# Batch 2's q^T by the DMA crossbar with batch 3's loads gated behind it, in place of batch 0's q in two halves

## The chip, the cores and the metric

The kernel runs on one core of a Trainium2 chip. The metric is the device time of one execution in microseconds (us). TensorE is called PE here (PEld its weight loads), VectorE DVE, ScalarE ACT, GpSimd POOL, SyncE SP. Loads from memory that also convert fp32 to fp16 are issued by POOL; output stores and crossbar transposes are issued by SP.

## The reference

Linformer attention, followed by a two-matrix maxout layer and an output projection:

```python
# q, k, v: (8 batches, 8 heads, 1024 tokens, 64); E, F: (64, 1024)
k_proj = np.einsum('ks,bhsd->bhkd', E, k)
v_proj = np.einsum('ks,bhsd->bhkd', F, v)
scores = scale * np.matmul(q, k_proj.transpose(0, 1, 3, 2))     # scale = 1/8
attn = np.exp(scores - max); attn = attn / (sum(attn) + 1e-09)
attn_out = np.matmul(attn, v_proj)

x = attn_out, heads side by side: (8192, 512)
h1, h2 = x @ w1, x @ w2                                         # (512, 1024) each
out = np.maximum(h1, h2) @ w_out                                # (1024, 512) -> float32
```

The kernel uses max(h1, h2) = relu(h1 - h2) + h2. So it needs the weight difference w1 - w2 (`wd_sb`), and a product M = w2 @ w_out (`m_sb`): out = relu(x @ wd) @ w_out + x @ M. From the second half of batch 0 on, both large products are made by a seven-product scheme on 2 x 2 blocks (p1 to p7 in the code).

## The kernel before

Tokens of a batch are split as 128 partitions x 8 blocks (`NC`). A tile of k, v or q holds a whole batch, 1 MB in fp16, and four such tiles rotate:

```python
kvq = ctx.enter_context(tc.tile_pool(name="kvq", bufs=4))
qtp = ctx.enter_context(tc.tile_pool(name="qtp", bufs=2))

def load(t, n, src, b, h0, h1, c0=0, c1=NC):
    nc.gpsimd.dma_start(
        out=t[n][:, h0:h1, c0:c1],
        in_=src[b, h0:h1].rearrange("h (p c) d -> p h c d", c=NC)[:, :, c0:c1],
    )
```

The first loads. Batch 0's q comes in two halves of the token blocks: the first among k's pieces, the second behind the first quarter of the weights:

```python
for h0 in (0, H // 2):
    for h in (h0, h0 + H // 4):
        load(tiles[0], "k", k, 0, h, h + H // 4)
    load(tiles[0], "q", q, 0, h0, h0 + H // 2, 0, NC // 2)
    ...
for h0 in (0, H // 2):
    load(tiles[0], "v", v, 0, h0, h0 + H // 2)
for f0 in range(0, DF, 256):
    for w_sb, w in ((w2_sb, moe_w2), (w1_sb, moe_w1)):
        for z in range(2):
            nc.gpsimd.dma_start(...)          # columns f0 to f0 + 256
    if f0 == 0:
        load(tiles[0], "q", q, 0, 0, H, NC // 2, NC)
nc.gpsimd.dma_start(out=wo_sb, ...)
```

Steps of attention. `step_kv` projects k and v with E and F on PE. `step_qt` turns q on PE and copies the result out of PSUM on DVE; `step_qt_dma` has the same done by the DMA crossbar; `step_gate` is a small POOL copy that keeps what POOL issues behind it until the named tile is there:

```python
def step_qt(t, h0, nh=2, i0=0, i1=NI, att=False):
    qt_ps = att_banks(FP16)[:, 0, :] if att else mm_bank(FP16)
    ...                                        # nh * (i1 - i0) transposes of 128 x 128
    nc.vector.tensor_copy(out=t["qt"][...], in_=qt_ps[...])

def step_qt_dma(t, h0=0, h1=H):
    nc.sync.dma_start_transpose(out=t["qt"][:, h0:h1]..., in_=t["q"][:, h0:h1]...)

def step_gate(t, n="kpt"):
    nc.gpsimd.tensor_copy(out=junk, in_=t[n][0:1, H - 1, 0:1])
```

`step_sc` makes scores and their exponentials for one group (g: four heads, j: half of the tokens), `step_dn` the sums of these and their logarithm on ACT, `step_inv` the inverse, `step_at` the values and the scaled result in `xt` (two multiplies on DVE). `step_wd` makes a quarter of w1 - w2 on DVE. `up_slots(t, j)` gives eight slots for half j of batch 0 (u0 and u1 below), each a block of 128 columns of relu(x @ wd); two slots share one quarter of wd. `step_w2t` turns w2, `step_m` makes M.

The head of the program, with `warm(n)` for n idle products that keep PE at work:

```python
step_kv(t, 0, 4, "k"); warm(2)
step_kpt(t, 0, 4); warm(2)
step_qt(t, 0, 4, 0, NI // 2); warm(2)
step_sc(t, 0, 0); warm(2)
step_kv(t, 4, 8, "k")
step_dn(t, 0, 0); step_inv(t, 0, 0); warm(2)
step_kpt(t, 4, 8); warm(4)
step_qt(t, 4, 4, 0, NI // 2); warm(2)
step_sc(t, 1, 0)
step_kv(t, 0, 4, "v")
step_dn(t, 1, 0); step_inv(t, 1, 0)
step_at(t, 0, 0); warm(4)
step_kv(t, 4, 8, "v")
step_at(t, 1, 0); warm(4)
step_wd(0)
load_all(tiles[1], 1, "k", k)

slots = [
    (0, u0[0]), (1, u0[1]), (None, f(step_qt, 0, 4, 2, 4)), (None, f(step_qt, 4, 4, 2, 4)),
    (None, wt[0]), (None, f(step_sc, 0, 1)), (None, f(step_sc, 1, 1)),
    (None, wd[1]), (2, u0[2]), (None, f(step_dn, 0, 1)), (None, f(step_inv, 0, 1)), (3, u0[3]),
    (None, f(step_dn, 1, 1)), (None, f(step_inv, 1, 1)), (None, wt[1]),
    (None, f(step_at, 0, 1)), (None, wd[2]), (4, u0[4]), (None, f(step_at, 1, 1)), (5, u0[5]),
    (None, lambda: loads(1, "v", "q", "k")), (None, wt[2]),
    (None, wd[3]), (6, u1[0]), (7, u1[1]), (8, u0[6]), (9, u0[7]), (None, wt[3]),
    (10, u1[2]), ...
    *((16 + n, lambda n=n: step_m(n)) for n in range(NDC)),
]
```

Then come the units, one for each half batch. A unit n works off the down products of half batch n (pieces "P"), the up products of half batch n + 1 (slots "U", n, h, i, with h the first or second half of the unit) and attention of a later batch in between (slots "G", n, h). Batch 1's attention stands in unit 0, batch 2's begins in unit 1:

```python
t = tiles[2]
at_slot(("P", 0, 6, 0), new_attn, t)
at_slot(("G", 1, 0), step_kv, t, 0, H, "kv", True)
at_slot(("G", 1, 0), loads, 3, "q", "v")
at_slot(("U", 1, 0, 1), step_kpt, t, 0, H, True)
for i, key in enumerate((("U", 1, 0, 0), ("U", 1, 0, 3), ("U", 1, 0, 5), ("U", 1, 1, 5))):
    at_slot(key, step_qt, t, 4 * (i % 2), 4, i // 2 * 2, i // 2 * 2 + 2, True)
for b in range(3, B):                          # n = 2 * b - 3
    at_slot(("G", n, 0), step_qt_dma, t, 0, H // 2)
    at_slot(("G", n, 0), step_qt_dma, t, H // 2, H)
    at_slot(("U", n, 0, 1), step_kv, t, 0, H, "kv", True, True)
    at_slot(("U", n, 0, 6), step_gate, t)
    at_slot(("U", n, 0, 6), loads, b + 1, "k", "v", "q")
```

The scores of batch 2's first group stand at slot ("G", 1, 1), those of its second at ("G", 2, 0).

Of the kernel before, what the change touches and what calls it, by code (L numbers as in the profile page):

```python
# [16 lines left out]
def kernel(  # L17
# [48 lines left out]
    def att_banks(dtype=FP32):  # L66
# [9 lines left out]
            name=nc.get_next_instruction_name(),  # L76
# [21 lines left out]
        alloc(t, n)  # L98
        load(t, n, src, b, 0, H)

    def load(t, n, src, b, h0, h1, c0=0, c1=NC):
        nc.gpsimd.dma_start(
            out=t[n][:, h0:h1, c0:c1],
            in_=src[b, h0:h1].rearrange("h (p c) d -> p h c d", c=NC)[:, :, c0:c1],
        )

    tiles = {b: {} for b in range(B)}
    for n in ("k", "q", "v"):
        alloc(tiles[0], n)
    for h0 in (0, H // 2):  # L110
        for h in (h0, h0 + H // 4):
            load(tiles[0], "k", k, 0, h, h + H // 4)
        load(tiles[0], "q", q, 0, h0, h0 + H // 2, 0, NC // 2)
        if h0 == 0:
            ident = const.tile([128, 128], FP32)
            make_identity(nc, ident)
    for h0 in (0, H // 2):
        load(tiles[0], "v", v, 0, h0, h0 + H // 2)

    w1_sb = big(1).rearrange("p (r f) -> p r f", r=NDC)  # L120
    w2_sb = big(2).rearrange("p (r f) -> p r f", r=NDC)
    wo_sb = const.tile([128, NFB, DM], FP16)
    for f0 in range(0, DF, 256):
        for w_sb, w in ((w2_sb, moe_w2), (w1_sb, moe_w1)):
            for z in range(2):
                nc.gpsimd.dma_start(
                    out=w_sb.rearrange("p (g z) f -> p g z f", z=2)[:, :, z, f0 : f0 + 256],
                    in_=w.rearrange("(g p z) f -> p g z f", p=128, z=2)[:, :, z, f0 : f0 + 256],
                )
        if f0 == 0:  # L130
            load(tiles[0], "q", q, 0, 0, H, NC // 2, NC)
    nc.gpsimd.dma_start(out=wo_sb, in_=moe_w_out.rearrange("(r p) f -> p r f", p=128))

    ones16 = const.tile([128, 512], FP16)
# [4 lines left out]
    def warm(n):  # L139
        w_ps = mm_bank()  # L140
        for _ in range(n):
            nc.tensor.matmul(  # L142
                out=w_ps, lhsT=ones16[:, 0:128], rhs=ones16, start=True, stop=True
            )
# [89 lines left out]
    def step_qt(t, h0, nh=2, i0=0, i1=NI, att=False):  # L234
        qt_ps = att_banks(FP16)[:, 0, :] if att else mm_bank(FP16)
        ni = i1 - i0
        for h in range(nh):
            for i in range(ni):
                nc.tensor.transpose(  # L239
                    out=qt_ps[:, (h * ni + i) * 128 : (h * ni + i + 1) * 128],  # L240
                    in_=t["q"][:, h0 + h, 2 * (i0 + i) : 2 * (i0 + i) + 2, :],
                    identity=ident16,
                )
        nc.vector.tensor_copy(
            out=t["qt"][:, h0 : h0 + nh, i0 * 128 : i1 * 128],
            in_=qt_ps[:, 0 : nh * ni * 128].rearrange("q (h n) -> q h n", h=nh),
        )
# [56 lines left out]
    def step_sc(t, g, j):  # L304
        sc_ps = att_banks()
        t["ps", g, j] = sc_ps
        score(t, g, j, [sc_ps[:, e, :] for e in range(2)])
        nc.scalar.activation(out=t["ex", g, j], in_=sc_ps, func=ACTF.Exp, scale=scale)

    def step_dn(t, g, j):  # L310
        dn_ps = t.pop(("ps", g, j))[:, :, 0:W]
        sums_into(t, g, j, dn_ps)
        t["ld", g, j] = soft.tile([128, 2, W], FP32, tag="ld", name="ld_sb")
        nc.scalar.activation(out=t["ld", g, j], in_=dn_ps, func=ACTF.Ln)

# [138 lines left out]
    U = {(b, o): {"n": n, "b": b, "o": o, "t": tiles[b]} for n, (b, o) in enumerate(units)}  # L454
# [260 lines left out]
    t = tiles[0]  # L715
# [4 lines left out]
    step_kpt(t, 0, 4)  # L720
    warm(2)
    step_qt(t, 0, 4, 0, NI // 2)
    warm(2)
    step_sc(t, 0, 0)
    warm(2)
    step_kv(t, 4, 8, "k")
    step_dn(t, 0, 0)
    step_inv(t, 0, 0)
    warm(2)
    step_kpt(t, 4, 8)  # L730
    warm(4)
    step_qt(t, 4, 4, 0, NI // 2)
    warm(2)
    step_sc(t, 1, 0)
    step_kv(t, 0, 4, "v")
    step_dn(t, 1, 0)
    step_inv(t, 1, 0)
    step_at(t, 0, 0)
    warm(4)
    step_kv(t, 4, 8, "v")  # L740
    step_at(t, 1, 0)
    warm(4)
    step_wd(0)


# [1 line left out]
    u0, u1 = [*up_slots(t, 0)], [*up_slots(t, 1)]  # L747
# [3 lines left out]

    def loads(b, *names):
        for n in names:
            b_ = b + (n == "k" and b < 3)
            if b_ < B:
                load_all(tiles[b_], b_, n, {"k": k, "v": v, "q": q}[n])

    slots = [
        (0, u0[0]), (1, u0[1]), (None, f(step_qt, 0, 4, 2, 4)), (None, f(step_qt, 4, 4, 2, 4)),
        (None, wt[0]), (None, f(step_sc, 0, 1)), (None, f(step_sc, 1, 1)),  # L760
        (None, wd[1]), (2, u0[2]), (None, f(step_dn, 0, 1)), (None, f(step_inv, 0, 1)), (3, u0[3]),
        (None, f(step_dn, 1, 1)), (None, f(step_inv, 1, 1)), (None, wt[1]),
        (None, f(step_at, 0, 1)), (None, wd[2]), (4, u0[4]), (None, f(step_at, 1, 1)), (5, u0[5]),
        (None, lambda: loads(1, "v", "q", "k")), (None, wt[2]),
        (None, wd[3]), (6, u1[0]), (7, u1[1]), (8, u0[6]), (9, u0[7]), (None, wt[3]),
        (10, u1[2]), (11, u1[3]), (12, u1[4]), (13, u1[5]), (14, u1[6]), (15, u1[7]),
        *((16 + n, lambda n=n: step_m(n)) for n in range(NDC)),
    ]
    slots = [((0, n), x) for n, x in slots]
# [25 lines left out]
    def at_slot(key, s, *a):  # L795
        steps.setdefault(key, []).append(lambda: s(*a))
# [14 lines left out]
    for n, x in enumerate((  # L811
        "kv", "", "kpt", "qt00 qt10", "", "sc00 qt01 qt11", "sc10", "dn00 in00", "sc01",
        "at00 dn10 in10", "sc11", "at10 dn01 in01", "dn11 in11", "at01", "at11",
    )):
        key = ("P", 0, (n - 1) // 2, (n - 1) % 2) if n else (0, 19)
        for name in x.split():
            if name[0] == "k":
                if name == "kpt":
                    at_slot(key, step_kpt, t, 0, H, True)
                else:  # L820
                    at_slot(key, step_kv, t)
                    at_slot(key, loads, 2, "v", "q")
            else:
                g, j = int(name[2]), int(name[3])
                s_ = {"qt": step_qt, "sc": step_sc,
                      "dn": step_dn, "in": step_inv, "at": step_at}[name[:2]]
                at_slot(key, s_, t, *((4 * g, 4, 2 * j, 2 * j + 2) if name[:2] == "qt" else (g, j)))
                if name == "qt11":
                    at_slot(key, loads, 2, "k")
        if n in (1, 5):  # L830
            at_slot(key, step_t, 1, (0, 1) if n == 1 else (2, 3))
        if 6 <= n < 10:
            at_slot(key, sums_x, U[0, 1], ((2, 0, 1, 3)[n - 6],))
# [2 lines left out]
    t = tiles[2]  # L836
    at_slot(("P", 0, 6, 0), new_attn, t)
    at_slot(("G", 1, 0), step_kv, t, 0, H, "kv", True)
    at_slot(("G", 1, 0), loads, 3, "q", "v")
    at_slot(("U", 1, 0, 1), step_kpt, t, 0, H, True)  # L840
    for i, key in enumerate((("U", 1, 0, 0), ("U", 1, 0, 3), ("U", 1, 0, 5), ("U", 1, 1, 5))):
        at_slot(key, step_qt, t, 4 * (i % 2), 4, i // 2 * 2, i // 2 * 2 + 2, True)
    for b in range(3, B):
        t = tiles[b]
        n = 2 * b - 3
# [74 lines left out]
```

## Time and profile before

| | |
|---|---|
| time, median of 3 runs | 338.49 us (336.88 to 339.25) |
| span of the profiled run | 335.1 us |
| busy PE, DVE, ACT, POOL | 322.6, 242.5, 201.6, 39.5 us |
| moved by DMA | 52.09 MB, 155 GB/s on average |
| granted PE clock | 1.00 in every slice |

The profile is of one execution. Its page cuts the span into 40 slices of about 8.4 us; a digit is the busy share of a slice in tenths. The chain is the work that ended last, followed back from the last instruction, by what released each step. A line of the timeline has the start, the duration, the engine (SPq: the queue of SP), the line of the program, the operation with its tiles, and in brackets how long the engine had been idle and what ended that. Time to landing of a DMA counts from its issue.

### The profile page before, as it was taken

The page shows a single profiled execution, that of the slowest core. Times are in us where ns is not written, and L with a number is a line of the kernel's source. Part 1 is how long each engine was busy: PE and PEld are TensorE (multiplying, and loading weights), DVE is VectorE, ACT ScalarE, POOL GpSimd, SP SyncE. Part 2 cuts the span into 40 slices and gives each one's busy share as a digit, 9 for nine tenths or more (in the row PEclk, how much of TensorE's full clock was granted, in tenths as well). Part 3 has the DMA queues.
Part 4 walks back from the last instruction along what each step waited for, and adds up shares of the span by engine and source line. Part 5 has one row for each costly group of instructions (what it writes and reads, how often), then busy time and mean ns, then how long its engine had stood idle before and what let it go on. Part 6 is the DMA issues. An engine that isn't in the chain of part 4 may idle for free.

```text
span 335.1 us, 9093 instructions
## 1 busy us (share of the span) xinstructions
PE 322.6 (96%) x3892; PEld 250.3 (75%) x3892; DVE 242.5 (72%) x430; ACT 201.6 (60%) x358; POOL 39.5 (12%) x58
## 2 busy tenths in 40 slices
PE   8977999999999999999999999999999999999994
PEld 3534446658888788877888788878887888888883
DVE  1354688988686779697878779677967796969572
ACT  2228422653577677766777677767776777764541
POOL 8558002102000030002100030003000000000000
PEclk9999999999999999999999999999999999999999
DMA  8999999999920969985999989996999320202032
GB/s 155 203 196 187 200 207 189 201 220 194 201 86 2 212 100 203 236 185 108 157 241 218 158 124 227 197 200 94 212 223 198 77 97 33 94 33 96 32 127 94
DMA packets 72616, 52.09 MB, mean 155 GB/s; under 512 B 25344, under 2 KB 72448, under 8 KB 72576
## 3 DMA queue, kind: packets, MB, share of 16 engines
q0 software_dynamic: 31472, 28.31, 54.2%
q1 hardware_dynamic: 41104, 23.21, 28.5%
q8 instruction: 30, 0.49, 0.5%
q14 instruction: 10, 0.08, 0.1%
HBM read 57.15 MB, written 16.78 MB: 221 GB/s over the span
## 4 chain that ended last, share of the span: by engine, by line
PE 90%; DVE 6%; issue 1%; ACT 1%; DVEq 0%
PE mm_ps L634 42%; PE mm_ps L556 25%; PE mm_ps L402 4%; PE att_ps L182 3%; PE att_ps L280 3%; PE mm_ps L142 3%; PE mm_ps L268 3%; PE mm_ps L438 2%; PE mm_ps L182 1%; DVE xt_sb L327 1%; PE mm_ps L239 1%; DVE o_sb L658 1%; PE mm_ps L280 1%; DVE gt_sb L571 1%; PE att_ps L268 1%
## 5 line engine op out<-in xcount | busy, mean ns | idle before, releaser
L527 ACT COPY p_sb<-mm_ps 128x512 f32<-128x512 f32 x172 | 97.3, 593 | 48.7 <-PE mm_ps L556 34.7
L634 PEld LDWEIGHTS <-big 128*128 128x128 f16 x768 | 73.2, 98 | 12.3 <-issue 3.7
L634 PE MATMUL mm_ps<-T_sb,big 128*128 128x256 f16 x576 | 78.1, 273 | 0.0
L571 DVE TENSOR_TENSOR gt_sb<-mm_ps,p_sb 128x512 f16<-128x512 f32 x56 | 38.5, 688 | 46.2 <-PE mm_ps L556 46.2
L556 PE MATMUL mm_ps<-big,big 128*128 128x256 f16 x336 | 50.4, 273 | 0.6 <-DVE gt_sb L571 0.6
L556 PEld LDWEIGHTS <-big 128*128 128x128 f16 x448 | 43.8, 98 | 5.8 <-issue 0.7
L634 PEld LDWEIGHTS <-gt_sb 128*128 128x128 f16 x384 | 35.5, 98 | 10.1 <-issue 5.8
L634 PE MATMUL mm_ps<-wo_sb,gt_sb 128*128 128x256 f16 x256 | 42.9, 273 | 0.1
L556 PEld LDWEIGHTS <-wd_sb 128*128 128x128 f16 x336 | 32.9, 98 | 4.2 <-issue 0.4
L556 PE MATMUL mm_ps<-xt_sb,wd_sb 128*128 128x256 f16 x224 | 33.6, 273 | 0.2 <-ACT ex_sb L353 0.2
L353 ACT ACTIVATE ex_sb<-mm_ps 128x512 f16<-128x512 f32 x48 | 26.1, 596 | 9.2 <-PE att_ps L280 7.0
L658 DVE TENSOR_TENSOR o_sb<-mm_ps,p_sb 128x512 f32<-128x512 f32 x32 | 21.9, 685 | 10.7 <-PE mm_ps L634 7.2
L379 DVE TENSOR_TENSOR xt_sb<-att_ps,ld_sb 128x1024 f16<-128x1024 f32 x24 | 29.3, 1219 | 0.1
L634 PE MATMUL mm_ps<-m_sb,xt_sb 128*128 128x256 f16 x128 | 24.4, 273 | 0.0
L606 ACT ACTIVATE gt_sb<-mm_ps 128x512 f16<-128x512 f32 x28 | 16.8, 600 | 8.7 <-PE mm_ps L556 8.7
L517 DVE TENSOR_TENSOR big<-gt_sb 128x1024 f16<-128x1024 f16 x32 | 21.9, 685 | 0.2
L231 POOL COPY junk<-kpt_sb 1x1 f16<-1x1 f16 x5 | 1.3, 251 | 174.4 <-DMA kpt_sb<-kp_sb 174.4
L574 DVE TENSOR_SCALAR gt_sb<-gt_sb 128x512 f16<-128x512 f16 (+1 forms) x56 | 20.3, 363 | 1.9
L634 PE MATMUL mm_ps<-wo_sb,big 128*128 128x256 f16 x128 | 21.5, 273 | 0.0
L634 PE MATMUL mm_ps<-T_sb,gt_sb 128*128 128x256 f16 x128 | 21.5, 273 | 0.0
L634 PEld LDWEIGHTS <-xt_sb 128*128 128x128 f16 x192 | 18.8, 98 | 2.2
L571 DVE TENSOR_TENSOR gt_sb<-p_sb 128x512 f16<-128x512 f32 x28 | 19.1, 682 | 0.0
(87 smaller groups left out, 443.8 us busy)
## 6 DMA issues: line engine op xcount, KB each, us to landing
out_dram<-o_sb SPq DMA_DIRECT2D x63, 256.0 KB, 2.6
k_sb<-in_k_dram POOLq DMA_DIRECT2D x7, 1024.0 KB, 10.7
v_sb<-in_v_dram POOLq DMA_DIRECT2D x7, 1024.0 KB, 17.3
q_sb<-in_q_dram POOLq DMA_DIRECT2D x7, 1024.0 KB, 21.9
big<-in_moe_w_dram POOLq DMA_DIRECT2D x16, 128.0 KB, 6.4
k_sb<-in_k_dram POOLq DMA_DIRECT2D x4, 256.0 KB, 6.3
v_sb<-in_v_dram POOLq DMA_DIRECT2D x2, 512.0 KB, 10.9
wo_sb<-in_moe_w_out_dram POOLq DMA_DIRECT2D x1, 1024.0 KB, 10.0
```

The source lines that it names most:

```text
L182: nc.tensor.matmul(out=kv_ps[r * KP : (r + 1) * KP, 0:n], lhsT=eft[:, i, c, :], rhs=t[w][:, h0:h1, c, :], start=(c == 0), stop=(c == NC - 1),)
L268: nc.tensor.matmul(out=banks[e][pos : pos + Z, h * W : (h + 1) * W], lhsT=t["kpt"][o * D : (o + 1) * D, head, s * Z : (s + 1) * Z], rhs=t[ ...
L353: nc.scalar.activation(out=t["ex", g, j][:, e, :], in_=banks[e], func=ACTF.Exp, scale=scale)
L379: nc.vector.tensor_tensor(out=x_out(t, g, j).rearrange("q z o n -> q o z n"), in0=at_ps.rearrange("q o (z n) -> q o z n", z=2), in1=ld[:, ...
L517: nc.vector.tensor_tensor(out=S(i), in0=x, in1=y, op=op)
L527: copy(out=x, in_=bank)
L556: nc.tensor.matmul(out=bank[:, m * W : (m + 1) * W], lhsT=w_[:, n_, (2 * d + m) * 128 : (2 * d + m + 1) * 128], rhs=a[:, n_, :], start=(n ...
L571: nc.vector.tensor_tensor(out=c_blk(j, c), in0=two(x), in1=two(y), op=ALU.add)
L574: nc.vector.tensor_scalar_max(ap, ap, 0.0)
L606: nc.scalar.activation(out=out, in_=in_, func=ACTF.Relu)
L634: nc.tensor.matmul(out=bank[:, i * CH : (i + 1) * CH], lhsT=a(c)[:, i * 128 : (i + 1) * 128], rhs=w_(c), start=(n is not None and m == (lo ...
L658: nc.vector.tensor_tensor(out=o_sb, in0=two(x), in1=two(y), op=ALU.add)
```

## The change

Two things are exchanged. Batch 0's q is loaded as a whole again, in four pieces among those of k, ahead of v; with it, both halves of the tokens go through transposes, scores and sums before the first weight difference, the weights come in two quarters and a half, and the slots behind are put in another order (u1 begins earlier). In unit 1, q of batch 2 is turned by the crossbar, as in the later batches, so that PE and DVE need not do it; and the three loads of batch 3, which were issued in unit 0 and at the start of unit 1, wait until that transpose has landed, so that the DMA engines are free for it.

```diff
     for h0 in (0, H // 2):
-        for h in (h0, h0 + H // 4):
-            load(tiles[0], "k", k, 0, h, h + H // 4)
-        load(tiles[0], "q", q, 0, h0, h0 + H // 2, 0, NC // 2)
+        for n, src in (("k", k), ("q", q)):
+            for h in (h0, h0 + H // 4):
+                load(tiles[0], n, src, 0, h, h + H // 4)
 ...
-    for f0 in range(0, DF, 256):
+    for f0, f1 in ((0, 256), (256, 512), (512, DF)):
 ...
-        if f0 == 0:
-            load(tiles[0], "q", q, 0, 0, H, NC // 2, NC)
 ...
     step_qt(t, 0, 4, 0, NI // 2)
+    step_qt(t, 0, 4, NI // 2, NI)
     warm(2)
     step_sc(t, 0, 0)
+    step_sc(t, 0, 1)
     warm(2)
     step_kv(t, 4, 8, "k")
     step_dn(t, 0, 0)
-    step_inv(t, 0, 0)
     warm(2)
     step_kpt(t, 4, 8)
+    step_dn(t, 0, 1)
+    step_inv(t, 0, 0)
     warm(4)
     step_qt(t, 4, 4, 0, NI // 2)
+    step_qt(t, 4, 4, NI // 2, NI)
     warm(2)
     step_sc(t, 1, 0)
+    step_sc(t, 1, 1)
     step_kv(t, 0, 4, "v")
     step_dn(t, 1, 0)
     step_inv(t, 1, 0)
     step_at(t, 0, 0)
-    warm(4)
+    step_dn(t, 1, 1)
+    step_inv(t, 0, 1)
     step_kv(t, 4, 8, "v")
+    step_inv(t, 1, 1)
     step_at(t, 1, 0)
-    warm(4)
     step_wd(0)
 ...
-            b_ = b + (n == "k" and b < 3)
+            b_ = b + (n == "k" and b < 2)
 ...
-        (0, u0[0]), (1, u0[1]), (None, f(step_qt, 0, 4, 2, 4)), (None, f(step_qt, 4, 4, 2, 4)),
-        (None, wt[0]), (None, f(step_sc, 0, 1)), (None, f(step_sc, 1, 1)),
-        (None, wd[1]), (2, u0[2]), (None, f(step_dn, 0, 1)), (None, f(step_inv, 0, 1)), (3, u0[3]),
-        ...
+        (0, u0[0]), (None, f(step_at, 0, 1)), (1, u0[1]), (None, f(step_at, 1, 1)),
+        (None, lambda: loads(1, "v", "q", "k")),
+        (None, wd[1]), (2, u1[0]), (3, u1[1]), (4, u0[2]), (None, wt[0]), (5, u0[3]),
+        (None, wd[2]), (None, wt[1]), (6, u1[2]), (7, u1[3]), (8, u0[4]), (9, u0[5]), (None, wd[3]),
+        (None, wt[2]), (10, u1[4]), (11, u1[5]), (12, u0[6]), (13, u0[7]), (None, wt[3]),
+        (14, u1[6]), (15, u1[7]),
 ...
-                if name == "qt11":
-                    at_slot(key, loads, 2, "k")
 ...
     at_slot(("G", 1, 0), step_kv, t, 0, H, "kv", True)
-    at_slot(("G", 1, 0), loads, 3, "q", "v")
     at_slot(("U", 1, 0, 1), step_kpt, t, 0, H, True)
-    for i, key in enumerate((("U", 1, 0, 0), ("U", 1, 0, 3), ("U", 1, 0, 5), ("U", 1, 1, 5))):
-        at_slot(key, step_qt, t, 4 * (i % 2), 4, i // 2 * 2, i // 2 * 2 + 2, True)
+    at_slot(("G", 1, 0), step_qt_dma, t, 0, H // 2)
+    at_slot(("G", 1, 0), step_qt_dma, t, H // 2, H)
+    at_slot(("U", 1, 0, 6), step_gate, t, "qt")
+    at_slot(("U", 1, 0, 6), loads, 3, "k", "v", "q")
```

More of the change, by code (lines that the diff above doesn't have):

```diff
@@ L99, in load_all, with load @@
         load(t, n, src, b, 0, H)
-    def load(t, n, src, b, h0, h1, c0=0, c1=NC):
+    def load(t, n, src, b, h0, h1):
         nc.gpsimd.dma_start(
-            out=t[n][:, h0:h1, c0:c1],
-            in_=src[b, h0:h1].rearrange("h (p c) d -> p h c d", c=NC)[:, :, c0:c1],
+            out=t[n][:, h0:h1],
+            in_=src[b, h0:h1].rearrange("h (p c) d -> p h c d", c=NC),
         )
@@ L116 @@
             make_identity(nc, ident)
-    for h0 in (0, H // 2):
-        load(tiles[0], "v", v, 0, h0, h0 + H // 2)
+    load(tiles[0], "v", v, 0, 0, H // 2)
+    load(tiles[0], "v", v, 0, H // 2, H)
     w1_sb = big(1).rearrange("p (r f) -> p r f", r=NDC)
@@ L126 @@
                 nc.gpsimd.dma_start(
-                    out=w_sb.rearrange("p (g z) f -> p g z f", z=2)[:, :, z, f0 : f0 + 256],
-                    in_=w.rearrange("(g p z) f -> p g z f", p=128, z=2)[:, :, z, f0 : f0 + 256],
-                )
-        if f0 == 0:
-            load(tiles[0], "q", q, 0, 0, H, NC // 2, NC)
+                    out=w_sb.rearrange("p (g z) f -> p g z f", z=2)[:, :, z, f0:f1],
+                    in_=w.rearrange("(g p z) f -> p g z f", p=128, z=2)[:, :, z, f0:f1],
+                )
     nc.gpsimd.dma_start(out=wo_sb, in_=moe_w_out.rearrange("(r p) f -> p r f", p=128))
@@ L758 @@
     slots = [
-        (0, u0[0]), (1, u0[1]), (None, f(step_qt, 0, 4, 2, 4)), (None, f(step_qt, 4, 4, 2, 4)),
-        (None, wt[0]), (None, f(step_sc, 0, 1)), (None, f(step_sc, 1, 1)),
-        (None, wd[1]), (2, u0[2]), (None, f(step_dn, 0, 1)), (None, f(step_inv, 0, 1)), (3, u0[3]),
[L762 to L766, printed above, removed]
+        (0, u0[0]), (None, f(step_at, 0, 1)), (1, u0[1]), (None, f(step_at, 1, 1)),
[4 more added lines that the diff above has]
+        (14, u1[6]), (15, u1[7]),
         *((16 + n, lambda n=n: step_m(n)) for n in range(NDC)),
```

## The prediction

> **What bounds the kernel now.** First the page: engine shares and the slices.
>
> ```profile
> PE 322.6 (96%) x3892; PEld 250.3 (75%) x3892; DVE 242.5 (72%) x430; ACT 201.6 (60%) x358; POOL 39.5 (12%) x58
> ...
> PE   8977999999999999999999999999999999999994
> ...
> DMA  8999999999920969985999989996999320202032
> ...
> PE 90%; DVE 6%; issue 1%; ACT 1%; DVEq 0%
> ```
>
> PE is busy in 96% of the span and carries 90% of the chain. It drops only in the first four slices (to about 33 us); there the DMA row stands at 9 and stays there until about 92 us. So the head waits for transfers and what hangs on them; behind it the kernel is as long as PE's queue. Hence the busy time by stage: from the first weight-difference product to the end of `step_m`, batch 1's attention, unit 1, and two later units of the steady state.
>
> ```profile
> 24.40:53.00 28.60, 26.16 (x226) 12.70 (x228) 19.16 (x33) 13.05 (x19) 7.89 (x10) 1.00 1.28 199
> 53.00:73.30 20.30, 19.63 (x322) 13.19 (x324) 18.06 (x34) 10.40 (x15) 2.63 (x3) 1.00 1.20 199
> 73.30:95.30 22.00, 21.26 (x264) 17.20 (x264) 17.36 (x34) 11.02 (x21) 1.75 (x2) 1.00 0.98 195
> 95.30:131.20 35.90, 35.90 (x459) 29.72 (x457) 27.36 (x49) 25.40 (x49) 2.81 (x4) 1.00 0.61 109
> ```
>
> Columns: stretch, length, busy PE, weight load, DVE, ACT, POOL, granted clock, DMA share, GB/s. Idle PE is length less PE: 2.44, 0.67, 0.74 and 0.00 us. The clock is 1.00 in all. The change can thus gain by taking PE instructions out of unit 1, by starting or filling the head better, and nowhere later. Then the timeline of PE in the head and in unit 1, with DVE and the queues:
>
> ```profile
> 24.42 1.90 PE L402 MATMUL mm_ps<-xt_sb,wd_sb 128*128 128x512 f16 x8 [1.12 <-DVE wd_sb L416]
> ...
> 34.20 1.04 PE L402 MATMUL mm_ps<-xt_sb,wd_sb 128*128 128x512 f16 x4 [2.09 <-DVE wd_sb L416]
> ...
> 79.32 0.68 DVE L244 COPY qt_sb<-att_ps 128x1024 f16<-128x1024 f16 x1
> ...
> 80.66 0.60 PE L556 MATMUL mm_ps<-big,big 128*128 128x256 f16 x4 [0.56 <-DVE gt_sb L571]
> 80.99 0.54 PEld L239 LDWEIGHTS <-q_sb 128*128 128x128 f16 x8
> ...
> 85.57 0.41 PE L268 MATMUL mm_ps<-qt_sb,kpt_sb 64*32 64x256 f16 x16
> ...
> 110.57 5.70 SPq L251 DMA_TRANSPOSE qt_sb<-q_sb  x2
> ```
>
> The 2.09 us gap at 34.20 is the largest behind 24.4: the third weight difference (`step_wd`) stands on DVE behind the late products of batch 0's second half. The 0.56 at 80.66 is DVE arriving late at `gt_sb` in unit 1, with a q^T copy of 0.68 just ahead of it. The last line is what the change asks for in unit 1, as batch 3 already has it.
>
> **What the Trainium skill says.** "TensorE: Matmul & The Clock Gate", Part 4: PE-mode transpose, says that a transpose on TensorE lands in PSUM and needs a DVE copy after it; the trace agrees: each eight of L239 have a 0.68 us copy of L244. "DMA: Bandwidth & Descriptors", Rules for kernel authors, says that a transpose next to ordinary DMAs needs nothing; so the gate on batch 3's loads serves time, not correctness. The same page, Issuing engines are not separate DMA queues, says that all queues end on the same 16 DMA engines and interleave; the trace agrees: a store landed in 2.2 to 2.5 us in the quiet stretch at 90 to 110 us and in 7 to 8 us beside loads at 61 to 79. That is why the gate matters.
>
> **Part one, batch 2's q^T in unit 1.** Removed: four `step_qt`, each 8 transposes on PE. The chain gives such a group 0.45 us (81.26, 83.45, 91.67), so 4 x 0.45 = 1.8 us of PE in a stretch where PE is the bound: all of it counts. Also removed: four DVE copies of 0.68, 2.7 us out of 17.36; off the path, but for the 0.56 gap that one of them helps to make: I count 0.4 of it. Added: two crossbar transposes on SyncE. Do they arrive in time? Batch 2's q is issued at 56.0 and takes 15.7 us to land (the issue's own row): 71.7, just before the slot at about 73. Nothing else is then queued on the loads' side, since k, v and q of batch 3 (issued at 62 and 75 before) now come later. The later pairs took 5.7 us for the first transpose and start 2 to 3 us apart, so from 71.5 to 73 the first half of heads lands at 77 to 79, the second at 79 to 81. The first score (L268) wanted it at 85.57, and comes some 3.5 us earlier now, at 82: 3 us to spare; the second half is wanted only one group later. The output stores behind it on SyncE's queue (78.50 the next) are clear.
>
> **Part two, the gate.** Batch 3's loads start at about 80 instead of 62 and 75. In the steady state the same three, issued from 121.2 on, had the last (q, 21.9 us from 122.9) landed at 144.8, so 23.6 us. From 80 that is 104. Batch 3's q was transposed from 110.57 and its kv projected at 113.65; less some 4 us saved, 106 and 109. Two us to spare, and a late transpose is still 4 us ahead of its score. So the gate costs nothing.
>
> **Part three, the head.** Gone is the splitting of q. All of q (1 MB as fp16) comes ahead of v; all four score groups of batch 0 stand before the first weight difference; eight warm-up products go, and the 16 transposes (0.89), 32 score products (about 0.9) and 16 sum products (about 0.5) that stood behind 24.4 move ahead of it: 2.3 us less PE work there. The price is a later start. The queue moves 1 MB in 5.1 us (k of batch 1 landed at 28.8 + 14.4 = 43.2, v at 29.6 + 18.6 = 48.2). By bytes, 3.0 MB were in by 21.3, 3.5 by 24.0. In the old order v's second half landed at 7.0 + 12.3 = 19.3; now 0.5 MB of q is ahead of it: 21.4. The first weight quarter moves from 21.3 to 24.0. From v on, in durations of the old trace: projection 1.06 to 22.8 with its copy to 23.2, value products to 23.7, two multiplies 1.29 to 25.1, weight difference 0.68 to 25.75. So the first product comes at 25.75, not 24.42: 1.3 later.
>
> Behind it 26.16 - 2.3 = 23.9 us of PE work remain. Idle: the order is u0[0], values (0,1), u0[1], values (1,1), u1[0]; the two pairs of multiplies on DVE (1.29 each) and PE's products run side by side, and u1[0] needs the last multiply: PE is done at 28.35, DVE at 29.75: 1.4 us. The later weight differences have no such wait: the third and fourth quarter, now one piece of rows twice as long, land at 32.3 by bytes, as the last quarter did before, and are wanted at 36. I add 0.4 for small waits. So `step_m` ends at 25.75 + 23.9 + 1.8 = 51.4 instead of 53.0: 1.6 earlier. Batch 1's v (landed 48.2) and q (53.3, wanted at about 55.5) are in by then, so the shift lasts.
>
> **Sum.** Head -1.6, unit 1's PE work -1.8, its gap -0.4: -3.8; with a little for other small gaps in unit 1 (0.74 idle in all), about -4.0. 338.5 - 4.0 = 334.5 us.
>
> **Rivals.** One: the head gets longer. The halves were there to bring v and the first weights sooner, and the first product is 1.3 us later; were the 2.3 us moved ahead not a gain, because the stage then idles on DVE or on the weights, the head would cost up to 1.3: 338.5 + 1.3 - 2.2 = 337.6. For it: DVE has 19.16 busy in 28.6 there and sits in each of PE's two large gaps. Against it: the 2.09 gap was caused by just those late products. Two: the crossbar is late, because q lands with nothing to spare (71.7 against 73) and stores share the engines. Past 82, each us late is a us of PE; at 3 us late the saving of part one is gone: 336.5 to 337. For it: the 15.7 us to landing. Against: the load that competed, k of batch 3, is now behind the gate. Three: the gate makes batch 3 late, its projection then standing at 109. If loads take 30 us instead of 23.6, 1 or 2 us go: 336. Four: DVE, lighter by 2.7 us in unit 1, frees more than I count: at most the rest of 0.74, so 334.
>
> **Range and chances.** The head is the widest term: from +0.5 to -3. Unit 1 is -2.2, with 1 us either way. The three times before spread 2.4 us, so I allow 1 for the measurement: 331.8 to 337.2. Two per cent faster would be 331.7, just outside: 0.11. Two per cent slower, 345.3, needs a transfer that is late by some 10 us: 0.03. Within: 0.86.
>
> **What would show it.** In the changed profile: PE matmuls fewer by the 32 transposes and 8 warm-up products, 3852 of 3892; the first weight-difference product at about 25.8 behind DVE; one gap of 1.4 before u1[0]; `step_m` done near 51.4; in unit 1 two crossbar transposes issued at 71 to 73, landing by 81, no PE wait for `qt_sb` or `kpt_sb`, and the stretch from batch 2's projection to unit 1's end shorter by 2.2; the gate released near 80, no wait in front of batch 3's projection; the later units as long as before (35.8 to 35.9 for two). What would make it wrong: a wait for weights in the head, a score of batch 2 released by the DMA, or a DVE that trails PE between 30 and 53 us.

## The result, and the profile after

The changed kernel takes 332.84 us (median of 4, 332.65 to 333.04), the kernel before 337.87 beside it (median of 4, 336.88 to 339.25): ratio 0.985, 95% interval 0.981 to 0.989. The spans of the profiled executions are 330.9 and 335.1 us, so 4.2 us are there to be found in the traces. The forecast was 334.5 for a kernel before at 338.5, a ratio of 0.988.

From the page of the changed kernel: the engines, then three rows of the slices (PE, granted PE clock, DMA).

```profile
PE 319.5 (97%) x3852; PEld 247.9 (75%) x3852; DVE 239.9 (73%) x426; ACT 201.4 (61%) x358; POOL 37.1 (11%) x56
...
PE   8968999999999999999999999999999999999994
...
PEclk9997999999999999999999999999999999999998
DMA  8999999998994979995998799996999321212132
```

3852 products, 40 fewer. The third slice of PE is lower than before (6 tenths instead of 7), the fourth higher (8 instead of 7); but the fourth has something new: a granted clock of 7 tenths. The same stages as before, cut at the same events (first weight-difference product, projection of batch 1, of batch 2, and the end of unit 1):

```profile
25.20:51.30 26.10, 25.06 (x160) 11.43 (x160) 18.30 (x32) 9.18 (x13) 4.25 (x5) 0.94 1.24 205
51.30:71.60 20.30, 19.64 (x321) 13.20 (x320) 17.85 (x33) 10.39 (x15) 1.76 (x2) 1.00 1.12 205
71.60:91.10 19.50, 19.32 (x231) 15.39 (x231) 14.56 (x30) 10.74 (x20) 2.90 (x4) 1.00 1.06 168
91.10:127.10 36.00, 36.00 (x460) 29.75 (x459) 27.36 (x49) 25.53 (x49) 2.81 (x4) 1.00 0.85 163
```

The first stage is 26.1 long instead of 28.6 and begins 0.9 later; its mean clock is 0.94. The second is as long as before, the third 2.5 shorter with almost no idle PE (0.18 instead of 0.74), the later units unchanged. So the head gives 1.6 and unit 1 gives 2.5. The timeline of the changed kernel at the places that the prediction named:

```profile
25.29 1.89 PE L400 MATMUL mm_ps<-xt_sb,wd_sb 128*128 128x512 f16 x4 [2.09 <-DVE wd_sb L414]
...
30.88 2.32 PE L400 MATMUL mm_ps<-xt_sb,wd_sb 128*128 128x512 f16 x10 [0.95 <-DVE xt_sb L325]
...
70.09 5.20 SPq L249 DMA_TRANSPOSE qt_sb<-q_sb  x2
...
78.03 0.26 POOL L229 COPY junk<-qt_sb 1x1 f16<-1x1 f16 x1 [22.75 <-DMA qt_sb<-q_sb]
...
82.00 0.41 PE L266 MATMUL mm_ps<-qt_sb,kpt_sb 64*32 64x256 f16 x16
```

Four products took 1.89 us at 25.29, where before eight took 1.90. The crossbar transposes were issued at 70.1 and had landed when the gate opened at 78.0; the score at 82.0 has no wait in its line.

All runs below are read by four marks of the profiled execution: the first weight-difference product, and the projections of batches 1, 2 and 3. "Head" is the time from the first mark to the second, "unit 1" from the third to the fourth, in us; this length takes in unit 2 as well, since batch 3's projection stands at the start of unit 3.

| kernel | first product | batch 1 | batch 2 | batch 3 | head | unit 1 | span |
|---|---|---|---|---|---|---|---|
| before | 24.42 | 52.92 | 73.22 | 113.65 | 28.50 | 40.43 | 335.1 |
| changed | 25.29 | 51.32 | 71.62 | 109.57 | 26.03 | 37.95 | 330.9 |
| head_only | 25.66 | 51.62 | 71.92 | 111.87 | 25.96 | 39.95 | 334.1 |
| unit1_only | 24.80 | 53.30 | 73.60 | 111.55 | 28.50 | 37.95 | 334.1 |
| no_gate | 27.98 | 52.60 | 72.90 | 122.03 | 24.62 | 49.13 | 343.3 |
| idle_pe | 25.32 | 51.22 | 71.53 | 111.17 | 25.90 | 39.64 | 333.1 |
| before_cold | 26.31 | 56.46 | 76.76 | 117.19 | 30.15 | 40.43 | 339.4 |
| warm8 | 26.81 | 52.17 | 72.44 | 110.39 | 25.36 | 37.95 | 332.5 |
| warm8_turn | 26.79 | 51.41 | 71.71 | 109.66 | 24.62 | 37.95 | 331.0 |
| kdup_only | 26.61 | 51.22 | 71.52 | 109.47 | 24.61 | 37.95 | 330.2 |
| fill_only | 27.45 | 50.29 | 70.59 | 108.54 | 22.84 | 37.95 | 329.8 |
| fill | 25.98 | 49.16 | 69.72 | 107.67 | 23.18 | 37.95 | 328.3 |
| fill_start | 26.21 | 49.06 | 69.36 | 107.31 | 22.85 | 37.95 | 328.0 |

The first mark wanders from execution to execution even where nothing ahead of it was changed (25.3 to 28.0 with the same first loads). The length of unit 1 does not: it is 37.95 in eight kernels. So lengths are compared, not spans. The head has two lengths for the same instructions, 24.6 and 25.9 to 26.0; the section on the clock takes that up.

### The profile page after: what moved, and what is told of

It is laid out like the page before. It is cut to its first block, busy times and chain, and to the rows that moved or that the text cites. A ratio compares the mean times of both kernels' runs of the same rounds, so it can differ in the third digit from the quotient of the medians.

```text
span 330.9 us, 9012 instructions
## 1 busy us (share of the span) xinstructions
PE 319.5 (97%) x3852; PEld 247.9 (75%) x3852; DVE 239.9 (73%) x426; ACT 201.4 (61%) x358; POOL 37.1 (11%) x56
## 4 chain that ended last, share of the span: by engine, by line
PE 87%; DMA 5%; DVE 4%; issue 1%; POOL 1%; ACT 0%; DVEq 0%; POOLq 0%
PE mm_ps L632 43%; PE mm_ps L554 25%; PE mm_ps L400 5%; PE att_ps L180 3%; DMA big<-in_moe_w_dram 3%; PE att_ps L278 3%; PE mm_ps L266 3%; DMA k_sb<-in_k_dram 2%; PE mm_ps L436 2%; DVE xt_sb L325 1%; DVE o_sb L656 1%; PE mm_ps L278 1%; DVE gt_sb L569 1%; POOL k_sb L102 1%; PE mm_ps L237 1%
## 5 line engine op out<-in xcount | busy, mean ns | idle before, releaser
L351 ACT ACTIVATE ex_sb<-mm_ps 128x512 f16<-128x512 f32 x48 | 26.1, 597 | 9.3 <-PE att_ps L278 7.0
L656 DVE TENSOR_TENSOR o_sb<-mm_ps,p_sb 128x512 f32<-128x512 f32 x32 | 21.9, 685 | 10.6 <-PE mm_ps L632 7.1
L400 PE MATMUL mm_ps<-xt_sb,wd_sb 128*128 128x512 f16 x64 | 16.3, 401 | 3.0 <-DVE wd_sb L414 2.1
```

The costliest lines, as they stand in the source:

```text
L351: nc.scalar.activation(out=t["ex", g, j][:, e, :], in_=banks[e], func=ACTF.Exp, scale=scale)
L400: nc.tensor.matmul(out=h_ps, lhsT=wd_sb[:, r, fb * 128 : (fb + 1) * 128], rhs=t["xt"][:, r, :, j * W : (j + 1) * W], start=(r == 0), stop= ...
L656: nc.vector.tensor_tensor(out=o_sb, in0=two(x), in1=two(y), op=ALU.add)
```

## The experiments

### One part alone: head_only and unit1_only

head_only is the changed kernel with unit 1 and the loads put back; unit1_only is the kernel before with these alone:

```diff
 # head_only, against the changed kernel
-            b_ = b + (n == "k" and b < 2)
+            b_ = b + (n == "k" and b < 3)
 ...
+                if name == "qt11":
+                    at_slot(key, loads, 2, "k")
 ...
+    at_slot(("G", 1, 0), loads, 3, "q", "v")
 ...
-    at_slot(("G", 1, 0), step_qt_dma, t, 0, H // 2)
-    at_slot(("G", 1, 0), step_qt_dma, t, H // 2, H)
-    at_slot(("U", 1, 0, 6), step_gate, t, "qt")
-    at_slot(("U", 1, 0, 6), loads, 3, "k", "v", "q")
+    for i, key in enumerate((("U", 1, 0, 0), ("U", 1, 0, 3), ("U", 1, 0, 5), ("U", 1, 1, 5))):
+        at_slot(key, step_qt, t, 4 * (i % 2), 4, i // 2 * 2, i // 2 * 2 + 2, True)
```

> The changed head (all of q ahead of v, new slot order) with unit 1 and batch 3's loads as in the kernel before. Theory (the two parts add up): the projection of batch 1 starts at about 51.3 us instead of 52.9, the stretch from batch 2's projection on is as in the kernel before, span about 333.5 us against 335.1 (-1.6). Rival (the gain is all in unit 1 and the head is only moved about): 335.1 again, -0.3 at most. If v or q of batch 1 and 2 become late without the gate's relief, more than 334.

> The kernel before with only unit 1 changed: crossbar transposes for batch 2, batch 3's loads gated behind them. Theory: head as before (projection of batch 1 at 52.9 us), the way from batch 2's projection to batch 3's crossbar transpose (73.2 to 110.6, 37.4 us) shorter by 2.5: span about 332.6 us. Rival (the crossbar pays only where the head is shorter, as q lands late at 71.7 in the old order): the first score waits for the transpose and the gain is 1 or less: 334 or more.

Measured: ratio to the kernel before 0.993 (0.990 to 0.997) for head_only, 0.995 (0.990 to 0.999) for unit1_only. The head alone brings batch 1's projection from 52.92 to 51.62, and unit 1 alone takes 2.48 off its stage, as in the changed kernel. The rival of unit1_only, a crossbar that is late in the old order, falls: its stage is 37.95 to the hundredth. At batch 3's projection the head alone is 1.78 us ahead of the kernel before, unit 1 alone 2.10, both together 4.08: the parts add up to within 0.2. Both spans came out worse than the marks, 334.1 each (333.5 and 332.6 were expected; 334 or more was the rival's figure for unit1_only), and the trace says why. In unit1_only:

```profile
227.99 0.41 PE L268 MATMUL mm_ps<-qt_sb,kpt_sb 64*32 64x256 f16 x16 [1.19 <-DMA kpt_sb<-kp_sb]
```

A score of a later batch waits 1.19 us for the crossbar transpose of the projected k. In head_only it is 0.90 at 156.3. In the changed kernel the five such transposes land 0.4 to 0.5 us ahead of their scores (the one issued at 149.72 took 2.72 us to land, 152.43, and the score started at 152.95), in the kernel before four of the five do (one took 3.38 us and landed only 0.04 ahead). When one takes 4.1 to 4.5 us instead of 2.7, PE waits. That happened once in each of the profiled executions of head_only, unit1_only, idle_pe, before_cold and warm8, thus with and without each part of the change, and belongs to neither.

One detail is new: unit 1 in head_only is 39.95, not 40.43. The gap of 0.56 behind DVE at 80.66 in the kernel before is absent there although the copies are not. Idle PE between the two marks is 0.74 us in the kernel before and 0.26 in head_only. So either part alone takes this gap away, and it can be counted to the head as well as to unit 1.

### What the gate is for: no_gate

```diff
-    at_slot(("U", 1, 0, 6), step_gate, t, "qt")
-    at_slot(("U", 1, 0, 6), loads, 3, "k", "v", "q")
+    at_slot(("G", 1, 0), loads, 3, "q", "v")
 ...                                              # k of batch 3 in unit 0, as in the kernel before
```

> The changed kernel without the gate: batch 3's loads are issued where the kernel before has them, k in unit 0, q and v at the start of unit 1, beside the crossbar transposes. Theory A (the gate matters): the transposes share the engines with 3 MB of loads, take 10 us or more instead of 4.4 to 5.5, and the first score of batch 2 (82.0 us now) waits for them: 1 to 3 us slower than the changed kernel, span 332 to 334. Theory B (the gate only removes slack): the transposes land later, at 78 to 81 us, but ahead of the score, and the span is 330.9 within 0.3.

Measured: 343.57 us, ratio 1.018 (1.012 to 1.023) to the kernel before: the change without its gate is a loss. Its timeline, SyncE's queue first:

```profile
71.59 18.86 SPq L249 DMA_TRANSPOSE qt_sb<-q_sb  x2
...
90.66 0.63 PE L266 MATMUL mm_ps<-qt_sb,kpt_sb 64*32 64x256 f16 x16 [7.31 <-DMA qt_sb<-q_sb]
91.22 1.04 PE L632 MATMUL mm_ps<-T_sb,big 128*128 128x256 f16 x4
...
102.24 0.41 PE L266 MATMUL mm_ps<-qt_sb,kpt_sb 64*32 64x256 f16 x16 [2.00 <-DVE big L515]
```

and the times from issue to landing of these two transposes, without the gate and, in the second fence, in the changed kernel:

```profile
DMA to landing us min/median/max: 19.0/21.1/23.1
```

```profile
DMA to landing us min/median/max: 4.4/4.9/5.5
```

The same transposes took 19.0 and 23.1 us beside the loads of batch 3 instead of 5.5 and 4.4. The issue on SyncE is held up too, 18.9 us for the pair instead of 5.2, with the output stores behind it. The first score waits 7.3 us. The wait of 2.00 at 102.24 is put down to a DVE instruction that had been done; the second transpose, issued at 79.06, landed at 102.19. Most of the other 1.9 goes with the clock:

```profile
82.00:88.00 6.00, 1.35 (x13) 0.97 (x10) 1.43 (x3) 1.09 (x2) 0.00 (x0) 1.00 1.43 104
88.00:95.00 7.00, 4.34 (x34) 2.87 (x35) 0.08 (x1) 2.15 (x4) 0.00 (x0) 0.52 1.26 176
95.00:102.00 7.00, 5.23 (x48) 4.42 (x45) 6.33 (x13) 2.84 (x5) 0.00 (x0) 1.00 1.26 151
```

After the idle stretch the clock is 0.52 on average from 88 to 95, and four products took 1.04 to 1.06 us instead of 0.60. Unit 1 is 49.13 instead of 37.95: 11.2 us, of which 9.3 are the two waits. Both theories fell short: A had the mechanism and a size of 1 to 3 us, B is refuted. Crossbar and loads together also move less than one after the other: without the gate 163 GB/s from 71.59 to 102.19, at a share of 1.30; with it, 187 GB/s from 70.09 to 101.95 in the changed kernel, at 1.04, for the transposes and then the three loads. The 104 GB/s from 82 to 88 prove less than that, since the changed kernel's transposes have a stretch of 74 GB/s at a share of 1.24 (72 to 74 us) with no load beside them. Why the two disturb each other so much stays open.

### PE's share in unit 1: idle_pe

The changed kernel with the 32 transposes of batch 2's q back in their four slots on PE, written to a PSUM bank that nothing reads; the copies on DVE stay out, the scores use the crossbar's result.

```diff
+    def step_qt_idle(t, h0, nh, i0, i1):      # the transposes of step_qt, without its copy
 ...
+    for i, key in enumerate((("U", 1, 0, 0), ("U", 1, 0, 3), ("U", 1, 0, 5), ("U", 1, 1, 5))):
+        at_slot(key, step_qt_idle, t, 4 * (i % 2), 4, i // 2 * 2, i // 2 * 2 + 2)
```

> The changed kernel with the 32 transposes of batch 2's q put back on PE in their four old slots, without the copies on DVE; their result is used by nothing. It measures PE's share of the gain in unit 1. Theory: all 1.8 us of it lie on the path: batch 2's projection to batch 3's (37.95 us in the changed kernel, 40.43 in the kernel before) becomes 39.7 to 39.8, and what is left to 40.43, 0.6 to 0.7, is the copies and the gap behind DVE. Rival (the copies on DVE were the bound of unit 1): 38.0 to 38.6.

Measured: unit 1 39.64, which is 1.69 more than 37.95; ratio to the kernel before 0.993 (0.991 to 0.996), against 0.985 for the changed kernel. The rival falls: the transposes are on the path with nearly their full time (1.8 by the four groups of 0.45). In time the difference is 0.8%, some 2.9 us; the two intervals allow 0.8 to 5.0, and the profiled execution has a late k^T of 0.7 in it. To 39.95, the stage with the old unit 1 behind the new head, 0.31 is left; it is put down to the copies as what remains, not by a run of its own. The other 0.48 to 40.43 is the gap that either part takes away.

### The clock in the head: before_cold, warm8, warm8_turn

The slices of the changed kernel showed a clock of 7 tenths in the fourth. In windows of 2 us:

```profile
24.00:26.00 2.00, 0.71 (x2) 0.28 (x3) 1.23 (x3) 0.06 (x1) 2.00 (x4) 0.75 1.38 201
26.00:28.00 2.00, 2.00 (x20) 0.43 (x19) 0.12 (x1) 0.60 (x1) 1.99 (x3) 0.50 1.24 204
28.00:30.00 2.00, 1.93 (x22) 0.60 (x21) 1.63 (x3) 0.60 (x1) 1.46 (x2) 0.90 1.23 203
```

Missing clock of 0.25, 0.50 and 0.10 over 2 us each is 1.7 us, so 3.4 us at one half. PE was busy for 0.68 us of 22 to 25. The Trainium skill, "TensorE: Matmul & The Clock Gate", Part 1: The HAM clock gate, says that the array's clock is halved after an idle window of about 3.4 us and that the window runs free, so that the moment varies from run to run; the trace agrees with the length and with the one half, but the stretch ahead of the fall was thin and not idle (below). The change dropped eight idle products there. First the other way round: the kernel before without them.

```diff
     step_at(t, 0, 0)
-    warm(4)
     step_kv(t, 4, 8, "v")
     step_at(t, 1, 0)
-    warm(4)
     step_wd(0)
```

> The kernel before without the two groups of four idle products behind the value products of batch 0's first half. Theory (PE loses its clock when these products go and it idles from 22 to 25 us): the granted clock falls to 0.50 for some 3.4 us from about 25 us on, the first eight weight-difference products take about 3.5 us instead of 1.9, and the projection of batch 1 starts 1 to 1.7 us later than 52.9. Rival (the fall in the changed kernel has to do with the new order, not with the idle products): clock 1.00 there and the start at 52.9 within 0.4.

```profile
24.00:26.00 2.00, 0.22 (x16) 0.00 (x0) 1.63 (x3) 0.00 (x0) 0.63 (x1) 1.00 1.45 194
26.00:28.00 2.00, 1.69 (x5) 0.59 (x6) 0.26 (x1) 0.00 (x0) 2.00 (x4) 0.57 1.44 193
28.00:30.00 2.00, 2.00 (x11) 0.90 (x10) 0.00 (x0) 0.69 (x2) 2.00 (x4) 0.58 1.37 183
```

The clock falls here too, for as long (0.43 and 0.42 of the clock missing over 2 us each, 1.7 again), and the head takes 30.15 instead of 28.50. The ratio is 1.003 (1.001 to 1.006), 1 us and so less than 1.65. Not every execution falls: of its 20, the four with a mean granted clock of 0.996 or 0.997 took 336.67 to 336.95 us, like the fastest of the kernel before beside it (336.73), the others 338.04 or more. Then the idle products put back into the changed kernel, eight of them where PE waits for the first weight difference; the second version also restores the order in which PSUM banks are taken:

```diff
     step_at(t, 1, 0)
+    warm(8)
+    turn.insert(0, turn.pop())        # warm8_turn only
     step_wd(0)
```

> The changed kernel with eight idle products put back behind the last value products, in the 2.1 us in which PE waits for the first weight difference. Theory (the granted clock fell to 0.50 at 25 us because the warm-up products were dropped): the clock stays 1.00, the first four products take 1.0 us instead of 1.9, the multiplies behind them start over 1 us earlier, and u1[0] starts at about 29.5 instead of 30.9: span about 329.5, 1.4 less than the changed kernel. Rival (u1[0] waits for the two pairs of multiplies on DVE anyway, so the slow clock is hidden): span 330.9 within 0.3.

> The changed kernel with the eight idle products in the wait for the first weight difference, now without moving the order of the PSUM banks (that made the projection of batch 1 wait 0.67 us for a copy on ACT in the first try). Theory: from the first weight-difference product to the projection of batch 1 26.0 us become 24.7 to 24.9 (25.36 in the first try, of which 0.67 was that wait), span 329.6 to 329.8 if the start is as in the changed kernel. Rival (hidden behind DVE): 25.8 or more.

warm8_turn's timeline:

```profile
24.64 1.90 PE L140 MATMUL mm_ps<-ones 128*128 128x512 f16 x8
26.79 1.04 PE L400 MATMUL mm_ps<-xt_sb,wd_sb 128*128 128x512 f16 x4 [0.26 <-DVE wd_sb L414]
```

Four products in 1.04 instead of 1.89, and a head of 24.62 against 26.03: 1.4 us, as the theory had it; "hidden behind DVE" is refuted. warm8 got only to 25.36 (ratio 0.987, 0.983 to 0.991), as its extra bank turn made the projection of batch 1 wait 0.7 us for the bank that a copy on ACT still held. In time little came of it, 332.38 us with a ratio of 0.985 (0.981 to 0.990), the changed kernel's: the first products are late in both profiled executions (26.8), for there PE ran at half speed from about 7 to 10.6 us, and the first projection of k took 1.9 us instead of 1.0 (the record of the granted clock shows 1.00 there; the durations of the products contradict it). That stretch of the program is the same in all these kernels, so the difference is one of executions.

One pair of profiles does not settle what the idle products do: kdup_only, whose head is the changed kernel's with none of them, had no fall of the clock at 25 us either, and a head of 24.61. The times of the falls do. Where a trace has several, they begin whole multiples of 3.41 us apart (before_cold at 9.21 and 26.28, five; no_gate at 9.72 and 88.22, 23), so stretches of this length follow each other at a position that differs between executions. The stretch just before the fall in the changed kernel and in idle_pe, then the thinnest of kdup_only around 25 us (counted back from its fall at 328.98) and that of warm8_turn (from 331.65):

```profile
21.58:24.99 3.41, 1.10 (x30) 0.56 (x24) 2.80 (x6) 1.63 (x3) 3.41 (x5) 1.00 1.44 196
22.81:26.22 3.41, 1.31 (x20) 0.45 (x20) 1.89 (x3) 1.15 (x3) 3.41 (x6) 1.00 1.40 196
21.79:25.20 3.41, 1.80 (x56) 0.97 (x40) 2.25 (x4) 2.44 (x5) 2.43 (x4) 1.00 1.44 195
21.04:24.45 3.41, 2.40 (x74) 1.51 (x69) 2.05 (x4) 2.50 (x5) 2.42 (x4) 1.00 1.44 193
```

Falls followed stretches with PE busy for 0.52 to 1.31 us (before_cold, the changed kernel, head_only, idle_pe), and none here followed 1.80 or more. The emptiest 3.41 us of the changed kernel hold 0.80 us of PE work (21.90 to 25.31), those of warm8_turn 2.40. So without the idle products the position of the stretches decides, and with them no position is as thin as those that lost the clock. The mean granted clocks of all executions, which leave out that early stretch, agree: 0.999 or 1.000 in 7 of 8 of warm8 and warm8_turn, 0.998 or more in only 4 of 31 of the changed kernel, head_only, idle_pe and kdup_only. Busy time is not the whole rule: at the start of the program the clock fell behind stretches with 2.2 to 2.7 us (no_gate, before_cold, fill_only).

What a fall costs, from the head of the changed kernel and that of kdup_only:

```profile
25.29:51.32 26.03, 25.08 (x161) 11.43 (x162) 18.28 (x31) 9.18 (x13) 4.16 (x5) 0.94 1.24 205
26.61:51.22 24.61, 23.72 (x161) 11.28 (x161) 18.28 (x31) 9.18 (x13) 4.13 (x5) 1.00 1.22 196
```

The same 161 products keep PE busy for 25.08 us instead of 23.72, and the heads take 25.90 to 26.03 in three profiles with the fall, 24.61 and 24.62 in two without (kdup_only, no_gate). But these two began their head later (26.61 and 27.98), and their batch 1 is projected at 51.22 and 52.60, no earlier than with the fall (51.22 to 51.62). So 1.4 us of the head are shown, and a gain in the whole time is not.

### A version that beats both: fill_only, kdup_only, fill, fill_start

PE's wait for the first weight difference can hold useful work. fill_only puts there the values of group (0,1), whose multiplies go behind the weight difference on DVE, the first quarter of the turn of w2, and three idle products; values (1,1) move ahead of u0[1]. kdup_only takes up the late k^T of the later batches: the second copy of the projected k goes ahead of the copy of v on DVE, so the transpose is issued earlier. fill is both, fill_start is fill with two more idle products in each of two places at the start.

```diff
 # fill_only
     step_at(t, 1, 0)
+    multiply_01 = step_at(t, 0, 1, later=True)
+    step_w2t(0)
+    warm(3)
+    turn.insert(0, turn.pop())
     step_wd(0)
+    multiply_01()
 ...
-        (0, u0[0]), (None, f(step_at, 0, 1)), (1, u0[1]), (None, f(step_at, 1, 1)),
+        (0, u0[0]), (None, f(step_at, 1, 1)), (1, u0[1]),
 ...
-        ... (4, u0[2]), (None, wt[0]), (5, u0[3]),
+        ... (4, u0[2]), (5, u0[3]),
 # kdup_only
-                nc.vector.tensor_copy(out=t["vp"][KP:128, h0:h1], in_=zd(kv_ps[KP:128, 0:n]))
                 if dma:
                     nc.vector.tensor_copy(out=kp[:, :, 1, :], in_=kp[:, :, 0, :])
                     step_kpt_dma(t)
+                nc.vector.tensor_copy(out=t["vp"][KP:128, h0:h1], in_=zd(kv_ps[KP:128, 0:n]))
 # fill_start, on top of both, behind the transposes of E and of F
-        warm(2)
+        warm(4)
```

> The filled head alone on the changed kernel, with the order of the copies of k and v in the later batches as it was. Theory: the projection of batch 1 at 49.2 us as in the full version (51.3 in the changed kernel), the units behind it 35.85 us each as in the changed kernel and not 35.72, span about 328.9; the k^T transposes land 0.4 us ahead of their scores, with a wait of 0.7 to 1.2 us in some executions.

> The changed kernel with only the copies swapped: the second copy of the projected k ahead of the copy of v. Theory: the k^T transposes land 1.0 to 1.2 us ahead of their scores instead of 0.4, no wait for k^T in front of a score, units of 35.72 us, span 330.3 to 330.9. Rival: no difference that can be seen in the span of the changed kernel, since its executions had no such wait.

> A kernel meant to beat both: the changed kernel with the wait for the first weight difference filled by useful work of PE, the values of group (0,1) and the first quarter of the turn of w2, and three idle products; the multiplies of (0,1) go behind the weight difference on DVE; and in the later batches the second copy of the projected k goes ahead of the copy of v, so that the k^T crossbar transpose is issued some 0.7 us earlier. Theory: clock 1.00, u1[0] at about 28.3 instead of 30.9, the projection of batch 1 at about 48.7 instead of 51.3, unless v of batch 1 (landed at 47.6) or its q (52.7) then becomes the bound; span about 328.5, time about 330.3. The k^T transposes land over 1 us ahead of their scores instead of 0.4. Rival (the weights or DVE set the end of the head): projection at 50.5 or later, span 330 or more.

> The best version so far with two more idle products behind each of the two groups of transposes of E and F at the start. In some executions (two of the profiled ones) the granted clock falls to 0.50 from 7 to 10 us, and the first projection of k starts at 9.1 instead of 8.1 and takes 1.9 us instead of 1.0. Theory (PE's work at 5 to 9 us is too thin to hold the clock): with four idle products there the clock holds in every execution, and the times scatter less, about 330.0. Rival (it depends on when the start falls and not on these few products): a later first projection of k, by 0.4 to 0.9 us, and a time 0.4 or more above the version without them.

| kernel | time, median of 4 | range | ratio to before |
|---|---|---|---|
| changed | 332.84 | 332.65 to 333.04 | 0.985 (0.981 to 0.989) |
| fill_only | 331.19 | 329.90 to 332.48 | 0.982 (0.979 to 0.986) |
| kdup_only | 332.82 | 331.95 to 336.18 | 0.989 (0.983 to 0.995) |
| fill | 330.29 | 329.42 to 331.08 | 0.979 (0.975 to 0.982) |
| fill_start | 329.73 | 329.55 to 330.36 | 0.978 (0.976 to 0.981) |

fill_only's interval overlaps the changed kernel's. The fill makes the head 22.84 to 23.18 instead of 24.6 (26.0 with the fall of the clock), in part because work went ahead of its first mark; batch 1's projection stands at 50.29, 49.16 and 49.06 instead of 51.3. What PE waits for in fill from 48 to 72 us (in total, how often, longest):

```profile
PE mm_ps L278 <- DVE xt_sb L327: 0.6, 2, 0.3
PE mm_ps L237 <- DMA q_sb<-in_q_dram: 0.2, 1, 0.2
```

The projection itself has no wait: batch 1's v landed at 48.7, 0.5 ahead of it (47.9, 1.2 ahead, in fill_start). Its q landed at 53.7, and the first transpose that reads it waits 0.2. So the head has nearly reached the loads, which stream without a break behind the weights, and more filling would gain 0.5 to 1.2 us at most until v holds it up. fill_only's execution started late (first product at 27.45, with a granted clock of 0.50 from 8.2 to 11.6), and its span is 329.8 and not 328.9.

kdup_only did what it was made for: in its profile and in those of fill and fill_start 14 of 15 k^T transposes land 0.9 to 1.2 us ahead of their scores (one, which took 3.3 us, 0.5), in fill_only 0.4 to 0.5. From batch 3's projection to the end the changed kernel takes 221.3 us, kdup_only and fill 220.7; from one batch's projection to the next it is 35.72 instead of 35.85 (two units; the expectations above call this a unit). Why that is 0.13 shorter stays open. In the time of kdup_only alone none of it can be told apart from the changed kernel; its rival stands as far as times go. fill_start is the fastest with the narrowest range, but the two intervals overlap nearly whole, and its first projection of k began at 9.06 instead of 8.22, as its rival had it; whether the four products hold the clock at the start in every execution is left open.

## Why the prediction was right, and where

**The head: the sum is right by luck, the terms are not.** The forecast was a first product at 25.75, 23.9 us of PE work and 1.8 of idle, so an end at 51.4. Measured: 25.29, 25.06 busy and 1.04 idle, an end at 51.3. "eight warm-up products go" was entered without a cost: that was the step that failed. Without them the clock can fall, as before_cold shows on the other kernel, and in this execution the fall added 1.36 us of busy PE; the PE work itself was forecast well, 23.72 us where the clock did not fall. The idle time was put too high by 0.8: PE waits 0.95 before u1[0] instead of 1.4, and of the 0.4 for small waits there is next to nothing. The slow products did not fill it, for it is 0.89 in kdup_only, without the fall, as well. And the first product came 0.5 earlier: v landed at 21.2 instead of 21.4, and in the working a projection of 1.06 us that starts at 21.4 ends at 22.8, where the sum gives 22.5. Without the fall of the clock the same head takes 24.6, which is 1.1 less than the 25.7 forecast. Rival one, a head that gets longer, did not happen: head_only gained. What each of the three changes in the head (q whole, the cut of the weights, the order of the slots) gives was not taken apart.

**Unit 1, PE: right.** 1.8 forecast, 1.69 by idle_pe. **The gap: right in size, less so in cause.** 0.4 to 0.6 forecast for DVE; 2.48 - 1.69 is 0.79, of which 0.31 is left for the copies and 0.48 is the gap behind DVE, which the new head takes away without any change in unit 1.

**The crossbar in time: right, with more to spare.** q was expected at 71.7 and the transposes at 77 to 79 and 79 to 81. The issue was at 70.1, and both had landed by 78.0; the first score came at 82.0 as forecast. Rival two did not happen in the changed kernel. But no_gate shows how near it lay: the step "the gate serves time" was right and far too small. Rival two priced a late transpose at up to 3 us; with loads beside it the price was 11.2. The Trainium skill, "DMA: Bandwidth & Descriptors", Rules for kernel authors, says that a transpose next to ordinary DMAs needs nothing, in a row about corrupted results; for time the measurement decides: 19.0 and 23.1 us instead of 5.5 and 4.4.

**The gate's price: right.** The loads of batch 3 were issued from 78.55 on (80 forecast); the transposes of batch 3's q went out at 106.50 (106 forecast) and its projection at 109.57 (109), with no wait in front of it. Rival three did not happen.

**Rival four**, a DVE that frees more, holds in part: idle PE in unit 1 fell from 0.74 to 0.18. The later units are unchanged, 35.85 us for two.

**The sum.** -4.0 was forecast and -4.2 is in the spans. The medians differ by 5.0, within their interval (0.981 to 0.989 is 3.8 to 6.5 us); the kernel before scatters by 2.4 us, and at least the waits for a late k^T transpose, up to 1.2 us, come and go between executions.

## What to carry to other kernels

A transfer that looks cheap in a quiet stretch has to be priced in the traffic of the stretch where it will stand; holding back the loads behind a gate was worth 11 us here, more than twice the whole gain. When idle "warm-up" products are dropped, look at the granted clock in the slices behind them, and put useful work or a few idle products into a wait of 2 us that follows a thin stretch. Compare lengths between marks inside the trace when the start of an execution wanders by more than the effect.

## What the runs showed of the hardware that was not expected

- Crossbar transposes beside loads: 19.0 and 23.1 us from issue to landing instead of 5.5 and 4.4, 163 GB/s moved over that stretch instead of 187 for the two one after the other, and SyncE's issue of the pair held for 18.9 us instead of 5.2.
- 3.41 us with PE busy for 0.5 to 1.3 of them were followed by a clock of one half over the next 3.41 us. These stretches lie at another position in each execution, so the same instructions lose the clock in some and not in others (26.0 or 24.6 us for the same head).
- A small k^T transpose that takes 2.7 us takes 4.1 to 4.5 now and then, and at a margin of 0.4 us PE waits 0.7 to 1.2 us for it.
